# Prefix of counts formed in PSUM, the last tile stored in two halves, and a new static order of instructions

## The chip, the cores and the metric

The kernel runs on one core of a Trainium2 chip. A core has five engines with instruction queues of their own: PE (TensorE, matmuls, operands from SBUF, results into PSUM banks), DVE (VectorE), ACT (ScalarE), POOL (GpSimd) and SP, which here only issues DMAs. PEld in the profile is PE's weight load. The metric is the device time of one execution, in microseconds.

## The reference

Attention over 8 batches with 8 heads (sequence 256, head dimension 64), then a gated depthwise convolution with 15 taps and SiLU, added to the attention's output; the sum is the input of a mixture of experts with 2048 tokens, 4 groups of 4 experts, one expert per token:

```python
scores = (q @ k.T) / sqrt(D); attn = softmax(scores); x = (attn @ v)    # (8, 256, 512)
x_g = x * sigmoid(glu_gate)
conv = depthwise_conv15(x_g, conv_w)                                    # same padding
x = x + conv * sigmoid(conv)                                            # (2048, 512) tokens
g = argmax(x @ w_group); e = argmax(x @ w_expert[g])
out = g_w * e_w * (relu(x @ w1[g, e]) @ w2[g, e])                       # F = 1024
```

`g_w` and `e_w` are the softmax values of the two choices. All arrays are fp32.

## The kernel before

**Tiling.** The attention and convolution run as 16 units: 4 groups of 2 batches, by 4 blocks of 128 channels (2 heads). Per unit: `pair` forms the scores (L490) and the product with v (L510), `head` the maximum (DVE, L519), the exponential (ACT, L524) and the transposes (PE, L531), `tail` the division and the gate. Units 1 to 5 take their convolution on PE (`conv_pe`): SP fetches shifted copies of the gated input (DMAs at L616), and L626 multiplies them with diagonals; the others take 15 taps on DVE (L671).

**Routing.** When a group's four units are done, `route` forms the logits on PE (L763, copied to SBUF, then L771), DVE picks group and expert (L787 to L813, result `oh`), PE counts them over the batch (L819), and DVE finds the expert that most of the batch's tokens want (its number `ei` is read by SP at L860) and the tokens that want another one (`ohl_all`). For those a place in a list is needed: `cum` is the running sum of `ohl_all` over the group's four tiles of 128 tokens (L836, L838), and L840 and L841 turn it into ranks. Meanwhile `rows` transposes x and writes its token rows to DRAM.

**Experts.** `dense` runs each batch of 256 tokens through its majority expert: 8 pieces of weights of 512 KB (`loads`, L865, into `raw` buffers, 5 of them), each split into a high part (`wh`, L293 from `split`, on ACT or DVE) and a rest (`wl`, two halves at L888, on POOL or DVE), then 96 matmuls of 128x256 (L914) for the first layer, relu with the same split (`hidden`, L948 to L961: `hh`, and `hl` either on DVE or by `tm` on ACT and POOL), 48 matmuls of 128x512 in two token tiles (L935 to L937), and `store` (scale by the router's weight at L973 or L975, one DMA of 256 KB at L978). Tokens that want another expert go through `leftover`: gathered rows, weights in `gv` slots (L1249, 8 slots of 512 KB, shared with the attention's inputs), two layers (L1169, L1192), and an indirect DMA by POOL (L1201, `scatter`) that writes them over the rows in `out`. Since it must come last for its rows, a scatter and the stores of `out` are ordered by the program. What is left after that goes through a loop with a dynamic count at the end (L1294), which has no round in these runs.

**What sets the order.** The instructions are emitted by a planner (`Flow`) while the program is built. Every stage is a generator that asks for an engine with a booked length (`run`, `at`), for a buffer (`get`, `take`) or for a flag; `Flow` keeps a queue for each engine and emits the ready entry of lowest key, with a planned time of its own. `KEYS` shifts the keys of stages, `WAYS` says instance by instance which engine takes a step that several can do, `SW` is the price in the key for a change of the matmul's shape on PE, and the constants NSL to CMO are numbers of buffers and caps on banks. So the order on each engine is fixed at build time, and a booked length or a key can move anything. `UC` is the number of L914 matmuls that are booked at a time.

Of the kernel before, what the change touches and what calls it, by code (L numbers as in the profile page):

```python
# [17 lines left out]
P = 128  # L18
# [25 lines left out]
NU = NG * NC  # L44
NSL = 22
HB = 3
NQK = 2
NGV = 8
NRAW = 5
NW = 4  # L50
# [3 lines left out]
KP = -4  # L54
CD = 598.26, 74.86, 138.82, 696.08
UC = 6
DC = 0
NPRO = 5
SW = 0.51
CSC = 6  # L60
CS0 = 4
CAC = 5
CMO = 7
NAV = 1
NPT = 6
NPR = 6
EXIT = 0.095
# [4 lines left out]
PC = 1, 2, 3, 4, 5  # L72
WAYS = dict(kk='1012001112122021', pT='1001100110101001000011001000100100000000000010001000100001000111', rb='22020221102202', rc='111100111010101', x='01001111110011', xg='0000100000000011', t1='11000000111011', silu='2001002110111221', res='00001010111', xh='01011010100001', xl='00010011', xr='0000010000011111', xd='011100100011101', ls='1001', wh='11000101001010001', wl='01000010000000110011101001000111000000000000011000000000000000000000000000001', y='00000011000001', yd='000100011111111', tap='1222101010000111', sb='0100001110011011', ab='110010000111', hl='10111111111110110010100101000011')
KEYS = dict(kk=2.03, score=-8.59, av=26.22, max=-9.5, exp=0.07, pT=71.65, dn=0.56, rt=-0.29, rc=1.94, xg=-21.49, cp=-6.47, th=-1.41, sp=-0.92, apt=0.31, conv=-1.17, convb=2.57, res=-0.53, xh=57.76, xl=-0.81, rows=1.68, lt=0.52, ls=-1.05, wh=9.13, hh=-0.67, hr=3.64, hm=1.04, y=-1.31, yd=0.81)
BOTH = "convb kk rb xg res xh xl wh wl".split()
# [201 lines left out]
def flag(f):  # L277
    return "flag", f
# [7 lines left out]
def attn_conv_moe(ctx, tc, aQ, aG, cw, wr, wE, cst, out):  # L286
# [185 lines left out]
    def pair(u, i):  # L472
# [12 lines left out]
        nm = small.tile([P, 2, 2], F32, name="nm")  # L485
        yield at("score", 0, u.k + 0.1 * i, ("PE", 0.875))
        for qt in range(2):
# [17 lines left out]
        if fl.now[2] < u.tv:  # L505
            fl.now[2], fl.now[3] = u.tv, None
        yield at("av", 0, u.k + 0.1 * i, ("PE", 0.875))
        for kt in range(2):
# [36 lines left out]
    def tail(u):  # L545
# [9 lines left out]
        v_.reciprocal(dn, dn)  # L555
        e = yield at("rb", u.n, u.k, ("ACT", 0.1 + 0.21 * nb), ("DVE", 0.07 + 0.14 * nb), ("POOL", 0.5 * nb))
        copy(e, rb[:, 0:nb].rearrange("p u (m d) -> p (u m) d", m=4),
# [141 lines left out]
    def residual(u, acc, ia):  # L699
# [12 lines left out]
        u.xl = slot(u.nl, F32R, u)  # L712
        e = yield at("xl", u.n, -3, ("POOL", 0.1 + 0.53 * nb), ("DVE", 0.1 + 0.27 * nb))
        on[e].tensor_tensor(u.xl, x, u.xh.bitcast(F32), ALU.subtract)
# [36 lines left out]
    def route(G_):  # L751
# [16 lines left out]
        lp, cp, rp = rt[:, 0:TT * 20], rt[:, 80:80 + nb * NE], rt[:, 112:112 + (TT + 1) * NE]  # L768
        yield run("PE", 0.85)
        for t in range(TT):  # L770
# [68 lines left out]
        yield run("PE", 0.5)  # L839
        t_.matmul(rp[:, 0:TT * NE], lt_ex, ohl, start=True, stop=False, skip_group_check=True)  # L840
# [38 lines left out]
    def split(m, n, ir, raw):  # L879
# [5 lines left out]
        for h in range(2):  # L885
            sl = slice(h * DM, h * DM + DM)
            e = yield at("wl", 16 * m.b + 2 * n + h, -1, ("POOL", 1.24), ("DVE", 0.63))
            on[e].tensor_tensor(wl[:, sl], raw[:, sl], wh[:, sl].bitcast(F32), ALU.subtract)  # L888
# [4 lines left out]
    def dense():  # L893
        for m in ms:
# [4 lines left out]
            for n in range(4):  # L899
# [7 lines left out]
                for f in range(2):  # L907
                    k = 0
                    for ww, lo in ((w4h, 0), (w4h, 1), (w4l, 0)):
                        for c in range(NC):  # L910
                            if k % UC == 0:
                                yield run("PE", 0.12 * UC)
                            x = (xs[c].xl if lo else xs[c].xh)[:, m.i, :]
# [4 lines left out]
            if m.i == gr[m.g].nb - 1:  # L918
                for u in xs:
                    fl.back("sl", u.nh)  # L920
                    fl.back("sl", u.nl)
            iy = yield take("bk", 2, "mo", CMO + 2 * (att[0] == NU))
            ys = [flat(bank(j)) for j in iy]
            for j in range(4):
# [5 lines left out]
                for t in range(2):  # L930
                    sl = slice(t * P, (t + 1) * P)
                    for k in range(2):
                        if DC or k == 0:
                            yield run("PE", 0.71 if DC else 1.42)
                        t_.matmul(ys[t], hh[:, k, sl], w3h[:, k, :], start=j == 0 and k == 0, stop=False)  # L935
# [7 lines left out]
    def hidden(m, n, ib, hp):  # L943
# [20 lines left out]
        fl.set(m.h[n])  # L964

    def store(m, t, iy, yp):
        yield flag(gr[m.g].done)
        n = yield get("y")
        y = work.tile([P, DM], F32, name="y", bufs=2)
        tt = 2 * m.b + t  # L970
        w = yield at("y", tt, -5, ("ACT", 0.55), ("DVE", 0.62))
        if w == "ACT":
# [119 lines left out]
    def gather_all(os):  # L1092
# [4 lines left out]
        for t0 in range(0, TA, 4):  # L1097
# [7 lines left out]
            yield run("PE", 0.45)  # L1105
            for t in range(4):
# [101 lines left out]
    def first_tables():  # L1208
# [4 lines left out]
        n = yield take("bk", 1, "lo")  # L1213
        yield run("DVE", 5.1)
        tables_a(flat(bank(n)))
# [140 lines left out]
```

## Time and profile before

| | us |
|---|---|
| median of 3 runs (369.4 to 369.95) | 369.69 |
| profiled execution | 370.42 |
| its span | 368.6 |
| PE busy in it | 348.4 (95%) |
| POOL busy | 266.2 (72%) |
| DVE busy | 280.8 (76%) |
| ACT busy | 232.2 (63%) |

The mean granted clock of PE was 0.989 of full speed. Up to about 240 us the attention and convolution overlap with the first expert batches; from 240 to 306 the leftover tokens and expert batches share PE, and the DMA engines are at their fullest; from 306.6 on there are only expert batches, until the last matmul ends at about 362.15.

### The profile page before, as it was taken

The page shows a single profiled execution, that of the slowest core. Times are in us where ns is not written, and L with a number is a line of the kernel's source. Part 1 is how long each engine was busy: PE and PEld are TensorE (multiplying, and loading weights), DVE is VectorE, ACT ScalarE, POOL GpSimd, SP SyncE. Part 2 cuts the span into 40 slices and gives each one's busy share as a digit, 9 for nine tenths or more (in the row PEclk, how much of TensorE's full clock was granted, in tenths as well). Part 3 has the DMA queues.
Part 4 walks back from the last instruction along what each step waited for, and adds up shares of the span by engine and source line. Part 5 has one row for each costly group of instructions (what it writes and reads, how often), then busy time and mean ns, then how long its engine had stood idle before and what let it go on. Part 6 is the DMA issues. An engine that isn't in the chain of part 4 may idle for free.

```text
span 368.6 us, 7954 instructions
## 1 busy us (share of the span) xinstructions
PE 348.4 (95%) x2766; PEld 277.0 (75%) x2766; DVE 280.8 (76%) x557; ACT 232.2 (63%) x534; POOL 266.2 (72%) x264
## 2 busy tenths in 40 slices
PE   7999999989999996998999999799999999999993
PEld 6666357635798776977787788779988977998982
DVE  3899948895999999999999999999999647201100
ACT  3987678746998653557989887344556534555521
POOL 1664766355887773569995866798869996999891
PEclk9999999999999998999999999899999999999999
DMA  7737964899266452549534332548999965855401
GB/s 269 246 117 177 305 225 150 198 322 325 97 238 218 166 195 77 203 132 339 217 115 172 116 114 88 199 136 288 412 409 390 371 249 186 307 195 181 163 2 64
DMA packets 29084, 77.13 MB, mean 209 GB/s; under 512 B 2999, under 2 KB 3255, under 8 KB 29041
## 3 DMA queue, kind: packets, MB, share of 16 engines
q1 hardware_dynamic: 27008, 72.94, 57.6%
q10 hardware_dynamic: 1872, 3.41, 2.5%
q8 instruction: 24, 0.39, 0.4%
q0 software_dynamic: 160, 0.23, 0.2%
q14 instruction: 20, 0.16, 0.1%
HBM read 63.67 MB, written 7.54 MB: 193 GB/s over the span
## 4 chain that ended last, share of the span: by engine, by line
PE 53%; DVE 25%; ACT 8%; DMA 6%; issue 4%; SPq 1%; POOL 1%; DVEq 0%; ACTq 0%; POOLq 0%
PE bk L914 19%; DVE bk L671 7%; PE bk L935 5%; PE bk L937 5%; PE bk L936 5%; ACT pr L524 5%; DVE nm L519 3%; PE bk L490 3%; PE bk L531 3%; PE bk L510 3%; DVE wl L888 3%; DMA gv<-wE 3%; PE bk L626 2%; DMA gv<-aG 2%; DMA wl<-sl 2%
## 5 line engine op out<-in xcount | busy, mean ns | idle before, releaser
L888 POOL TENSOR_TENSOR wl<-raw,wh 128x512 fp32r<-128x512 f32 x113 | 145.3, 1311 | 12.4 <-ACT wh L293 11.6
L671 DVE SCALAR_TENSOR_TENSOR bk<-sl,cwq,bk 128x512 f32<-128x512 f32 x143 | 102.6, 747 | 1.3
L914 PE MATMUL bk<-sl,wh 128*128 128x256 f32 x512 | 79.2, 294 | 0.0
L293 ACT CAST wh<-raw 128x1024 fp32r<-128x1024 f32 x57 | 60.1, 1054 | 23.9 <-PE bk L937 11.7
L914 PEld LDWEIGHTS bk<-sl,wh 128*128 128x128 f32 x512 | 68.5, 195 | 5.3 <-issue 3.9
L524 ACT ACTIVATE pr<-bk,nm 128x256 f32<-128x256 f32 x128 | 59.4, 493 | 19.4 <-DVE nm L519 18.9
L935 PE MATMUL bk<-wh,hh 128*128 128x512 f32 x128 | 51.8, 405 | 0.0
L936 PE MATMUL bk<-wl,hh 128*128 128x512 f32 x128 | 50.6, 395 | 0.0
L937 PE MATMUL bk<-wh,hl 128*128 128x512 f32 x128 | 50.6, 395 | 0.0
L519 DVE TENSOR_REDUCE nm<-bk 128x2 f32<-128x512 f32 x64 | 40.1, 681 | 8.3 <-PE bk L490 8.2
L961 POOL TENSOR_TENSOR hl<-tm,hh 128x512 fp32r<-128x512 f32 x20 | 27.0, 1352 | 19.8 <-ACT tm L954 14.8
L914 PE MATMUL bk<-sl,wl 128*128 128x256 f32 x256 | 41.4, 285 | 0.0
L531 PE MATMUL bk<-c_id,pr 128*128 128x128 f32 x256 | 36.2, 278 | 4.1 <-ACT pr L524 4.0
L948 ACT ACTIVATE hh<-bk 128x512 fp32r<-128x512 f32 x32 | 19.3, 603 | 31.7 <-PE bk L914 21.8
L531 PEld LDWEIGHTS bk<-c_id,pr 128*128 128x128 f32 x256 | 28.2, 140 | 13.1 <-ACT pr L524 8.3
L914 PEld LDWEIGHTS bk<-sl,wl 128*128 128x128 f32 x256 | 35.6, 193 | 0.0
L490 PE MATMUL bk<-qk 64*128 64x256 f32 x256 | 32.9, 392 | 0.1
L510 PE MATMUL bk<-pT,gv 128*64 128x256 f32 x256 | 32.7, 388 | 0.0
L490 PEld LDWEIGHTS bk<-qk 64*128 64x128 f32 x256 | 23.4, 186 | 7.4 <-issue 4.4
L524 ACT ACTIVATION_READ_ACCUMULATOR pr<-bk,nm 128x1 f32 x128 | 28.8, 225 | 0.0
L935 PEld LDWEIGHTS bk<-wh,hh 128*128 128x128 f32 x128 | 24.1, 188 | 5.9 <-issue 0.8
L937 PEld LDWEIGHTS bk<-wh,hl 128*128 128x128 f32 x128 | 24.1, 188 | 5.8
(161 smaller groups left out, 550.5 us busy)
## 6 DMA issues: line engine op xcount, KB each, us to landing
raw<-wE SPq DMA_DIRECT2D x64, 512.0 KB, 4.5
gv<-wE SPq DMA_DIRECT2D x24, 512.0 KB, 10.0
gv<-aG SPq DMA_DIRECT2D x16, 512.0 KB, 5.7
qk<-aQ SPq DMA_DIRECT2D x15, 512.0 KB, 3.7
wh<-sl SPq DMA_DIRECT2D x10, 270.0 KB, 6.1
wl<-sl SPq DMA_DIRECT2D x10, 270.0 KB, 5.7
out_dram<-y SPq DMA_DIRECT2D x9, 256.0 KB, 4.4
out_dram<-y ACTq DMA_DIRECT2D x7, 256.0 KB, 3.0
```

The costliest lines, as they stand in the source:

```text
L293: (a_.copy if e == "ACT" else on[e].tensor_copy)(o, i)
L490: t_.matmul(scs[hh][:, qt, :], t[sl, i, qt * P:(qt + 1) * P], t[sl, i, 256:512], start=True, stop=True)
L510: t_.matmul(u.a[64 * hh:64 * hh + 64, i, :], u.vt[:, i, kt, hh, :], pTs[hh][1][:, kt, :], start=kt == 0, stop=kt == 1)
L519: v_.reduce_max(nm[:, hh, :], sc, axis=AX.X, negate=True)
L524: a_.activation(pr[:, qt, :], sc[:, qt, :], AF.Exp, bias=nm[:, hh, qt:qt + 1], scale=1.0, accum_out=u.sm[:, i, qt, hh, 0:1])
L531: t_.transpose(tp[:, kt, qt * P:(qt + 1) * P], pr[:, qt, kt * P:(kt + 1) * P], ident)
L671: v_.scalar_tensor_tensor(acc if k == KT - 1 else ac, x, w, acc if k == m and m > 1 else ac, ALU.mult, ALU.add)
L888: on[e].tensor_tensor(wl[:, sl], raw[:, sl], wh[:, sl].bitcast(F32), ALU.subtract)
L914: t_.matmul(hp[:, f, :], ww[:, f, c, :], x, start=k == 0, stop=k == 11)
L935: t_.matmul(ys[t], hh[:, k, sl], w3h[:, k, :], start=j == 0 and k == 0, stop=False)
L936: t_.matmul(ys[t], hh[:, k, sl], w3l[:, k, :], start=False, stop=False)
L937: t_.matmul(ys[t], hl[:, k, sl], w3h[:, k, :], start=False, stop=j == 3 and k == 1)
```

## The change

- `route`: the copy and the three adds of the running sum go into the routing's PSUM bank (`sums`), and one copy takes the result to SBUF as `cum`, which L841 (now L843) reads as before.
- `dense`: for the last 128 tokens (last batch, second tile) each 128x512 matmul becomes two of 128x256, one for each half of the columns, in banks of their own (three banks instead of two in the last batch). `half` scales the first half on DVE and stores it by SP, the second on ACT and by ACT's queue, 128 KB each.
- Buffers: `raw` 5 to 3, `gv` 8 to 10, slots for x (`NSL`) 22 to 23, exponentials (`NPR`) 6 to 4.
- The planner: `UC` 6 to 12, `SW` 0.51 to 75.59, the caps CSC and CAC, new `WAYS` and `KEYS`, and other booked lengths in some twenty places (the conv units' DMAs among them).

The units on PE are 1 to 5 in both. The core of the diff (lines of `KEYS` and `WAYS` cut):

```diff
-NSL = 22
+NSL = 23
...
-NGV = 8
-NRAW = 5
+NGV = 10
+NRAW = 3
...
-UC = 6
+UC = 12
...
-SW = 0.51
+SW = 75.59
-CSC = 6
+CSC = 5
...
-CAC = 5
+CAC = 2
...
-NPR = 6
+NPR = 4
...
-        yield run("SP", 2.4, -20)
+        yield run("SP", 4.3, -20)
...
-        fl.now[2] = max(fl.now[2] + 3.2, fl.land(1200))
+        fl.now[2] = max(fl.now[2] + 4.3, fl.land(1800))
...
-        yield run("DVE", 1.45)
+        yield run("DVE", 1.65)
...
         cum = small.tile([P, TT, NE], F32, name="cum")
-        v_.tensor_copy(cum[:, 0], ohl[:, 0])
+        sums = ps(0, TT, NE)
+        v_.tensor_copy(sums[:, 0], ohl[:, 0])
         for u in range(1, TT):
-            v_.tensor_tensor(cum[:, u], cum[:, u - 1], ohl[:, u], ALU.add)
-        yield run("PE", 0.5)
+            v_.tensor_tensor(sums[:, u], sums[:, u - 1], ohl[:, u], ALU.add)
+        v_.tensor_copy(cum, sums)
...
-            iy = yield take("bk", 2, "mo", CMO + 2 * (att[0] == NU))
+            iy = yield take("bk", 3 if m.b == B - 1 else 2, "mo", CMO + 2 * (att[0] == NU))
...
+                    if m.b == B - 1 and t == 1:
+                        if j == 3:
+                            yield get("y")
+                            y = work.tile([P, DM], F32, name="y", bufs=2)
+                        for h in range(2):
+                            yield run("PE", 0.71)
+                            c, yp = slice(h * S, h * S + S), ys[1 + h][:, 0:S]
+                            for k in range(2):
+                                t_.matmul(yp, hh[:, k, sl], w3h[:, k, c], start=j == 0 and k == 0, stop=False)
+                                t_.matmul(yp, hh[:, k, sl], w3l[:, k, c], start=False, stop=False)
+                                t_.matmul(yp, hl[:, k, sl], w3h[:, k, c], start=False, stop=j == 3 and k == 1)
+                            if j == 3:
+                                fl.go(half(m, h, c, y, yp), -5, fl.now[2], "PE")
+                        continue
...
+    def half(m, h, c, y, yp):
+        yield flag(gr[m.g].done)
+        tt = 2 * m.b + 1
+        yield run(("DVE", "ACT")[h], (0.35, 0.33)[h])
+        if h:
+            a_.activation(y[:, c], yp, AF.Copy, scale=rec[:, tt, 1:2])
+        else:
+            v_.tensor_scalar(y[:, c], yp, rec[:, tt, 1:2], None, ALU.mult)
+        w = ("SP", "ACT")[h]
+        yield run(w, 0.43)
+        on[w].dma_start(out=out[tt * P:(tt + 1) * P, c], in_=y[:, c])
```

How the order moves is shown at two places. The first is DVE's queue where the second group is routed; `L787` is its first step of the choice and `L671` are conv taps (numbers behind `bk` and `sl` name banks and slots). Before:

```order
L888 TENSOR_TENSOR wl<-raw,wh 128x512
L293 CAST wh<-raw 128x1024
L671 SCALAR_TENSOR_TENSOR bk_1631<-sl_995,cwq,bk_1631 128x512
L671 SCALAR_TENSOR_TENSOR bk_1765<-sl_1198,cwq,bk_1765 128x512
L671 SCALAR_TENSOR_TENSOR bk_1631<-sl_995,cwq,bk_1631 128x512
L787 TENSOR_REDUCE gmx<-bk_1767 128x4
```

and after, where `bk_1814` is the routing's bank and the copy is that of the logits:

```order
L671 SCALAR_TENSOR_TENSOR bk_1545<-sl_999,cwq,bk_1545 128x512
L293 COPY y<-bk_1814 128x512
L671 SCALAR_TENSOR_TENSOR acc<-sl_999,cwq,bk_1545 128x512
L671 SCALAR_TENSOR_TENSOR bk_1885<-sl_1205,cwq,bk_1885 128x512 x2
L787 TENSOR_REDUCE gmx<-bk_1814 128x4
```

A weight subtraction and a weight cast left this place on DVE, and the logits' copy came to it.

The second is the end of the program. On ACT, whose last work is the last y, before:

```order
L293 CAST wh<-raw 128x1024 x2
L948 ACTIVATE hh<-bk_4599 128x512
L954 ACTIVATE tm<-bk_4599 128x512
L973 ACTIVATE y<-bk_4632,rec 128x512
L973 ACTIVATE y<-bk_4633,rec 128x512
L978 DMA out_dram<-y 128x512
```

and after (`bk_4121` holds a leftover tile's second layer, `ys` its scaled rows):

```order
L964 ACTIVATE hh<-bk_4545 128x512
L293 CAST wh<-raw 128x1024
L1001 ACTIVATE y<-bk_4579,rec 128x512
L987 ACTIVATE y<-bk_4581,rec 128x256
L992 DMA out_dram<-y 128x256
L1225 ACTIVATE ys<-bk_4121,sws 128x128
```

On PE the same end, after (L942 to L944 are the half-width matmuls, L1220 is the leftover's second layer, L1192 before):

```order
L944 MATMUL bk_4581<-wh,hl 128x256
L942 MATMUL bk_4581<-wh,hh 128x256
L943 MATMUL bk_4581<-wl,hh 128x256
L944 MATMUL bk_4581<-wh,hl 128x256
L1220 MATMUL bk_4121<-gv,hT 32x128 x32
```

The last leftover product moved from ahead of the last group's routing to the end of PE's queue, behind the last tile's halves; its `ys` and the scatter are the last work of ACT and POOL, and the scatter waits there for the stores of the last tile.

## Rows read from the trace of the kernel before

**Rows 1.** The page's busy times: us, share of the span, instructions.

```profile
PE 348.4 (95%) x2766; PEld 277.0 (75%) x2766; DVE 280.8 (76%) x557; ACT 232.2 (63%) x534; POOL 266.2 (72%) x264
```

**Rows 2.** Windows: stretch, length, busy time of engines, clock, DMA share, GB/s.

```profile
240.00:306.60 66.60, 65.64 (x771) 57.35 (x770) 55.71 (x106) 33.28 (x50) 59.05 (x48) 1.00 0.82 312
306.60:362.20 55.60, 55.19 (x333) 48.46 (x332) 11.44 (x35) 26.00 (x34) 49.40 (x40) 1.00 0.51 172
```

**Rows 3.** Waits of PE: line, waited for, us in total, times, longest.

```profile
PE bk L531 <- ACT pr L524: 4.0, 8, 1.2
PE bk L819 <- DVE oh L813: 3.0, 2, 2.8
PE bk L841 <- DVE cum L838: 2.2, 2, 1.9
PE bk L626 <- DMA wh<-sl: 1.6, 2, 1.3
PE bk L378 <- POOL sm L432: 1.0, 1, 1.0
PE bk L1169 <- DMA gv<-wE: 1.0, 1, 1.0
```

**Rows 4.** Timeline: start, us, engine and line; in brackets idle time before, releaser.

```profile
137.59 1.76 DVE L293 CAST wh<-raw 128x1024 fp32r<-128x1024 f32 x1
139.28 2.06 DVE L671 SCALAR_TENSOR_TENSOR bk<-sl,cwq,bk 128x512 f32<-128x512 f32 x3
...
144.34 0.63 PE L819 MATMUL bk<-oh,c_sb 128*128 128x32 f32 x4 [2.79 <-DVE oh L813]
...
167.33 2.48 DVE L519 TENSOR_REDUCE nm<-bk 128x2 f32<-128x512 f32 x4
...
169.12 0.66 PE L531 MATMUL bk<-c_id,pr 128*128 128x128 f32 x4 [1.18 <-ACT pr L524]
...
230.02 2.63 DVE L838 TENSOR_TENSOR cum<-cum,ohl_all 128x16 f32<-128x16 f32 x3
```

**Rows 5.** Windows behind two of the waits; the third last number is the clock.

```profile
145.10:148.50 3.40, 3.40 (x17) 3.40 (x18) 3.19 (x10) 1.77 (x3) 2.83 (x3) 0.51 0.41 154
233.90:237.20 3.30, 3.30 (x18) 3.30 (x17) 2.88 (x15) 2.02 (x3) 2.09 (x2) 0.50 0.80 266
```

**Rows 6.** Groups by form: shapes and count, busy us, mean ns, idle before.

```profile
L838 DVE TENSOR_TENSOR cum<-cum,ohl_all 128x16 f32<-128x16 f32 x12 | 6.2, 517 | 0.4
L836 DVE COPY cum<-ohl_all 128x16 f32<-128x16 f32 x4 | 3.0, 754 | 0.1
L789 DVE TENSOR_TENSOR bk<-bk,c_sb 128x16 f32<-128x16 f32 x8 | 1.5, 182 | 0.3
```

**Rows 7.** DMA issues from 246 to 302, then from 306 to 350: median us to landing.

```profile
gv<-wE SPq DMA_DIRECT2D x24, 512.0 KB, 10.0
raw<-wE SPq DMA_DIRECT2D x11, 512.0 KB, 9.5
...
raw<-wE SPq DMA_DIRECT2D x16, 512.0 KB, 4.3
```

**Rows 8.** Groups by form, the cast and the subtraction of the weights.

```profile
L293 ACT CAST wh<-raw 128x1024 fp32r<-128x1024 f32 x57 | 60.1, 1054 | 23.9 <-PE bk L937 11.7 <-PE bk L914 3.5 <-POOL wl L888 3.4
L888 POOL TENSOR_TENSOR wl<-raw,wh 128x512 fp32r<-128x512 f32 x113 | 145.3, 1311 | 12.4 <-ACT wh L293 11.6 <-DVE wh L293 0.8
```

**Rows 9.** The chain that ended last: start, us, what.

```profile
301.01 1.89 PE bk L1192 x64
...
362.19 0.69 ACT y L973
```

**Rows 10.** DMA issues from 355 to 369: count, KB each, median us to landing.

```profile
out_dram<-y SPq DMA_DIRECT2D x1, 256.0 KB, 2.1
out_dram<-y ACTq DMA_DIRECT2D x1, 256.0 KB, 3.0
out_dram<-ys,ixs POOLq DMA_INDIRECT x1, 2.1
```

More of the change, by code (lines that the diff above doesn't have):

```diff
@@ L54 @@
 KP = -4
-CD = 598.26, 74.86, 138.82, 696.08
-UC = 6
+CD = 870.39, 381.01, 464.81, 600.18
+UC = 12
 DC = 0
 NPRO = 5
-SW = 0.51
-CSC = 6
+SW = 75.59
+CSC = 5
 CS0 = 4
-CAC = 5
+CAC = 2
 CMO = 7
@@ L72 @@
 PC = 1, 2, 3, 4, 5
[L73 to L74 removed]
+WAYS = dict(kk='1012020202222211', pT='110001011011000000100000011000000000010001000000000000000101', rb='1222022200022212', rc='10111001100001', x='001000000010001', xg='000111000100101', t1='0011000111111001', silu='0222211112120012', res='0011100000000001', xh='0110001000110001', xl='11010000111', xr='0101000100000011', xd='0111101011001111', ls='0101', wh='001000000000001', wl='11000000000100000000101000000000000010001010001001', y='01000000001', yd='1110100011111111', tap='21121401110041', sb='0000000001111111', ab='1000010001010111', hl='0101101100010110011001000000001')
+KEYS = dict(kk=-1.0, tg=-7.8, score=-78.01, max=-2.23, exp=1.28, tp=-4.53, pT=-0.08, rb=0.58, rt=-1.9, rc=0.58, x=-1.93, xg=0.96, cp=0.03, th=-5.5, sp=-1.16, apt=-2.18, conv=0.45, convb=-0.61, res=-15.34, xh=1.39, xl=-2.75, xr=-4.43, lt=0.67, wl=2.54, hh=2.67, hr=3.07, y=0.23, yd=0.26)
 BOTH = "convb kk rb xg res xh xl wh wl".split()
@@ L485, in pair @@
         nm = small.tile([P, 2, 2], F32, name="nm")
-        yield at("score", 0, u.k + 0.1 * i, ("PE", 0.875))
+        yield at("score", 0, u.k + 0.1 * i, ("PE", 0.87))
         for qt in range(2):
@@ L506, in pair @@
             fl.now[2], fl.now[3] = u.tv, None
-        yield at("av", 0, u.k + 0.1 * i, ("PE", 0.875))
+        yield at("av", 0, u.k + 0.1 * i, ("PE", 0.87))
         for kt in range(2):
@@ L555, in tail @@
         v_.reciprocal(dn, dn)
-        e = yield at("rb", u.n, u.k, ("ACT", 0.1 + 0.21 * nb), ("DVE", 0.07 + 0.14 * nb), ("POOL", 0.5 * nb))
+        e = yield at("rb", u.n, u.k, ("ACT", 0.1 + 0.21 * nb), ("DVE", 0.07 + 0.14 * nb), ("POOL", 0.28 * nb))
         copy(e, rb[:, 0:nb].rearrange("p u (m d) -> p (u m) d", m=4),
@@ L712, in residual @@
         u.xl = slot(u.nl, F32R, u)
-        e = yield at("xl", u.n, -3, ("POOL", 0.1 + 0.53 * nb), ("DVE", 0.1 + 0.27 * nb))
+        e = yield at("xl", u.n, -3, ("POOL", 0.1 + 0.57 * nb), ("DVE", 0.1 + 0.27 * nb))
         on[e].tensor_tensor(u.xl, x, u.xh.bitcast(F32), ALU.subtract)
@@ L768, in route @@
         lp, cp, rp = rt[:, 0:TT * 20], rt[:, 80:80 + nb * NE], rt[:, 112:112 + (TT + 1) * NE]
-        yield run("PE", 0.85)
+        yield run("PE", 0.82)
         for t in range(TT):
@@ L816, in route @@
         o4 = oh.rearrange("p (i t) e -> p t i e", i=nb)
-        yield run("PE", 0.5)
+        yield run("PE", 0.4)
         for t in range(2):
@@ L835, in route @@
         cum = small.tile([P, TT, NE], F32, name="cum")
-        v_.tensor_copy(cum[:, 0], ohl[:, 0])
+        sums = ps(0, TT, NE)
+        v_.tensor_copy(sums[:, 0], ohl[:, 0])
         for u in range(1, TT):
-            v_.tensor_tensor(cum[:, u], cum[:, u - 1], ohl[:, u], ALU.add)
-        yield run("PE", 0.5)
+            v_.tensor_tensor(sums[:, u], sums[:, u - 1], ohl[:, u], ALU.add)
+        v_.tensor_copy(cum, sums)
+        yield run("PE", 0.42)
         t_.matmul(rp[:, 0:TT * NE], lt_ex, ohl, start=True, stop=False, skip_group_check=True)
@@ L886, in split @@
             sl = slice(h * DM, h * DM + DM)
-            e = yield at("wl", 16 * m.b + 2 * n + h, -1, ("POOL", 1.24), ("DVE", 0.63))
+            e = yield at("wl", 16 * m.b + 2 * n + h, -1, ("POOL", 1.25), ("DVE", 0.63))
             on[e].tensor_tensor(wl[:, sl], raw[:, sl], wh[:, sl].bitcast(F32), ALU.subtract)
@@ L911, in dense @@
                             if k % UC == 0:
-                                yield run("PE", 0.12 * UC)
+                                yield run("PE", 0.1185 * UC)
                             x = (xs[c].xl if lo else xs[c].xh)[:, m.i, :]
@@ L931, in dense @@
                     sl = slice(t * P, (t + 1) * P)
+                    if m.b == B - 1 and t == 1:
[12 more added lines that the diff above has]
+                        continue
                     for k in range(2):
                         if DC or k == 0:
-                            yield run("PE", 0.71 if DC else 1.42)
+                            yield run("PE", 0.705 if DC else 1.41)
                         t_.matmul(ys[t], hh[:, k, sl], w3h[:, k, :], start=j == 0 and k == 0, stop=False)
@@ L970, in store @@
         tt = 2 * m.b + t
-        w = yield at("y", tt, -5, ("ACT", 0.55), ("DVE", 0.62))
+        w = yield at("y", tt, -5, ("ACT", 0.58), ("DVE", 0.65))
         if w == "ACT":
@@ L1104, in gather_all @@
                              io32.unsqueeze(1).broadcast_to([P, 4, m]), ALU.is_equal)
-            yield run("PE", 0.45)
+            yield run("PE", 0.62)
             for t in range(4):
@@ L1213, in first_tables @@
         n = yield take("bk", 1, "lo")
-        yield run("DVE", 5.1)
+        yield run("DVE", 5.5)
         tables_a(flat(bank(n)))
```

## Prediction

> **What bounds the kernel now.** I read the busy times first: TensorE (PE) is busy 95% of the span, VectorE (DVE) 76%, ScalarE (ACT) 63% [rows 1]. By stretches, PE has 65.64 us of work in the 66.6 us from 240 to 306.6 and 55.19 in the 55.6 after that [rows 2]. PE's instructions are the same before and after but for 24 matmuls that become 48 of half the width, so time can only come from PE's waits, from stretches at the lower clock, and from the tail behind the last matmul. The waits of PE are the second view: eight groups, 13.4 us in all, the six of a microsecond or more in [rows 3]. The third view is the granted clock: behind the wait of 2.79 us at 144.34 [rows 4] and behind the longest wait for `cum`, 1.9 us [rows 3], the clock reads 0.51 and 0.50 for 3.40 and 3.30 us, with PE busy throughout [rows 5]. That is the 1.2 GHz level, and half of each stretch is lost: 3.4 us. Behind the waits of 1.0 to 1.3 us no such stretch follows. So 13.4 + 3.4 = 16.8 us is the most that a better order could give back ahead of the tail.
>
> **The change part by part.**
>
> *Routing, the choice of the expert.* In the second group's routing PE waits 2.79 us for `oh`. The timeline shows why [rows 4]: the logits are there at about 137.8, and DVE then has the cast of 1.76 us (from 137.59) and three conv taps (2.06 us) to end before it can start on the choice at 141.3, some 3.4 us late. In the new order the cast is gone from that place; behind the copy of the logits stand three taps alone, and they run while PE still folds the logits (L771). 1.76 us of cast go, and some 0.6 of the taps come under L771: 2.4 of the 2.79. The other `oh` wait (3.0 - 2.79 = 0.2) goes with it. Term: **-2.6**. The cast isn't lost: ACT takes five more of 1.05 us each [rows 8], spread over the run, and it is idle 37% of it.
>
> *Prefix of counts.* Before, `cum` is a copy of 754 ns and three adds of 517 ns, by the means, in SBUF [rows 6]; the three took 2.63 us in the third group's routing [rows 4], where L841 waits 1.9. After, copy and adds write PSUM. The nearest row is L789, the same shape, with one operand and the result in a bank: 182 ns [rows 6]. With 0.2 for each of the two copies it is 0.2 + 3 x 0.18 + 0.2 = 0.9 us against 2.3 by the means and about 3.4 in the third group: 1.4 to 2.5 us less. From the other side: adds of 517 ns kept and a copy put on top, +0.2. I take L789's value, since engine, shape and places are the same. L841 waits 2.2 us in two routings; PE also has somewhat more rows between L819 and this matmul than before in every routing. Term: **-2.2**.
>
> *The clock.* Both half-clock stretches come behind these two waits, so they go with them: **-3.4**; nothing, if new waits of that length appear elsewhere.
>
> *Conv units on PE.* Their matmuls wait 1.6 us in two places for the shifted copies that SP fetches [rows 3]. The planner now books 4.3 us of SP for them and a landing at least 4.3 us off, instead of 2.4 and 3.2, and in the new order each unit's first L626 stands behind 1 to 6 us more PE work than before. Term: **-1.4**, 0.2 kept.
>
> *Leftover weights.* Ten `gv` slots for eight, and the leftover matmuls stand 5 to 10 us of PE work later. The one wait for them is 1.0 us [rows 3]. Term: **-1.0**. The two slots more let 512 KB loads start earlier in a stretch where a load takes 10.0 us to land already [rows 7]; that is weighed with the raw buffers.
>
> *Softmax.* L531 waits 4.0 us in eight places [rows 3], the longest, at 169.12, for an exponential that stood behind 2.48 us of maxima on DVE [rows 4]. DVE has fewer weight casts (7 to 2), fewer weight subtractions (15 to 10), a shorter prefix, and more of `hl` (12 to 20). I take a quarter: **-1.0**, bounds 0 and -2.
>
> *Three raw buffers for five.* A piece of weights goes load, cast on ACT (1.05), two subtractions on POOL (2 x 1.31) [rows 8], then its buffer is free. With 9.5 to 10 us of landing between 246 and 302 [rows 7] a round trip is 10 + 1.05 + 2.6 + 0.5 = 14.2 us, or 4.7 a piece with three buffers; the eight pieces of that stretch have 5.1 us of PE work each to hide under by the new order. So it costs nothing while the round trip is under 15.4 us, and then about 8 / 3 = 2.7 us for each microsecond. After 306 a load lands in 4.3 [rows 7]: 8.5 / 3 = 2.8 us a piece, about what POOL needs anyway. Term: 0; it is the main rival.
>
> *The last tile.* Before, the last matmul ends at about 362.15, and 6.4 us follow: ACT's y (0.69 us from 362.19) [rows 9], the store (3.0 us from issue to landing) [rows 10], 2.7 to the program's end. After, its columns come as two halves of 128 KB, scaled by DVE and ACT, stored by SP and ACT. PE's work for it stays (as many columns), and the third bank that it takes is free, attention being over; were it not, PE would wait for one y, 0.69. And the last leftover product, 1.89 us of PE that stood at 301.01 [rows 9], now stands behind all dense matmuls, its `ys` and its scatter last of all. The scatter waits on POOL, with no work queued behind it, for the landing of the last y stores. So the dense part ends 1.9 us sooner, and behind it come 0.1, half a y (between half of 0.69 and all of it: 0.5), a store, the scatter (2.1) [rows 10] and the 2.7. The store of a half lies between 1.5 (half of 3.0) and 3.0; I take 2.7, near the rows of whole tiles, since none shows time falling with size. 0.1 + 0.5 + 2.7 + 2.1 + 2.7 = 8.1, less 1.9 is 6.2, against 6.4. Term: **-0.2**, bounds -1.4 and +0.1.
>
> Here rows and a rule part. The two 256 KB stores at the end land 2.1 and 3.0 us after their issue [rows 10], so the rows leave open what a half costs. The Trainium skill (DMA: Bandwidth & Descriptors, section "Anatomy of one DMA — SWDGE (gpsimd) path") fits a transfer as about 2.0 us fixed plus bytes at 436 GB/s, which makes a half 2.3 us by estimate, so that splitting brings next to nothing. By that fit the tail's term is -0.6 instead of -0.2, and the forecast 0.4 lower. It is fitted on a software queue, and these stores go by hardware queues, so the rows stand.
>
> *New waits.* Choices and keys change for every stage, so the whole order is new. Bounds: no wait, and as much as the old order had, 16.8. Where they will lie the trace of before can't show; the measure I take is what the old order had apart from routing, conv and leftover loads (L531 4.0, L378 1.0): **+5**.
>
> **Sum.** -2.6 - 2.2 - 3.4 - 1.4 - 1.0 - 1.0 - 0.2 + 5 = -6.8. The profiled execution took 370.42 us, so 363.6; it lay 0.73 above the median of the runs, 369.69, so **362.9**.
>
> **The rivals.**
>
> *The waits come back elsewhere.* For it: DVE is the busiest engine behind PE, and its queue decides most of the waits. Against it: the largest have causes that the new order removes. With 12 for 5 the sum is +0.2: 369.9, no change.
>
> *Slower: three raw buffers starve PE in the stretch full of loads.* Place: 246 to 302, where `gv` and `raw` loads share the DMA engines, 82% busy over the wider window [rows 2, 7]; ten `gv` slots put more of them ahead of each raw load. It decides from a round trip of 15.4 us; at 18.5 it costs 3.1 x 2.7 = 8.4 us, and a half-clock stretch that such waits bring 1.7: 362.9 + 8.4 + 1.7 = 373.0. Against it: fewer loads in flight land sooner.
>
> *A new long wait, and the clock behind it.* The first dense chunk of the first group now stands behind 10 us of PE work from L819, where it had 18. The expert's number must be formed and read by SP, then the load takes 4.3 or more, the cast 1.05, a subtraction 1.31 [rows 7, 8]: 6.7 and what the number takes. A wait of 2 us and a half-clock stretch are 3.7: 366.6.
>
> *The prefix in PSUM is no faster.* Then L841's 2.2 and one half-clock stretch stay: +3.9, 366.8.
>
> **How the numbers follow.** The forecast, 355.7 to 367.5: 0.60. Waits come back, around 369.9: 0.13 (0.04 faster, 0.05 the same, 0.04 slower). Raw buffers, 371 to 377: 0.14. Long wait: 0.09, prefix: 0.04, both faster. The low end is the sum with no new waits, 357.9, and the lower bounds of the softmax and tail terms, 2.2 less. The high end, 371, takes in the first rival and the mildest of the second. Faster 0.60 + 0.04 + 0.09 + 0.04 = 0.77; same 0.05; slower 0.18. Within 0.2% (0.74 us) a measurement can't tell this kernel from no change.
>
> **What would show it.** PE's wait at the second group's L819 under 0.6 us, and for `cum` under 0.4 in every routing; copies and adds of `cum` under 0.25 us each; no window at half clock after 100; no wait of L626 over 0.5; the last y store landing 2.1 to 3.0 us after its issue, and the scatter right behind it. I am wrong if landing, cast and subtractions of a raw piece exceed 15.4 us between 240 and 300 and PE waits for `wh` or `wl` there, or if PE's waits come to more than 10 us again.

## The result, and the profile after

The changed kernel takes 358.04 us (median of 4 runs, 357.0 to 360.25) against 369.57 for the kernel before: a ratio of 0.9695, 95% interval 0.9648 to 0.9741. The forecast was 362.9 with a range of 355.7 to 371.0; the sign and the range held, and the gain was 11.5 us where 6.8 were forecast.

The busy times of the profiled execution (358.33 us, span 356.6), to be held against [rows 1]:

```profile
PE 342.7 (96%) x2790; PEld 272.1 (76%) x2790; DVE 268.9 (75%) x554; ACT 236.7 (66%) x537; POOL 257.6 (72%) x257
```

PE's busy time itself fell by 5.7 us, though it has the same work but for the last tile's halves. The waits of PE in the changed kernel, against [rows 3] (line, waited for, total, times, longest):

```profile
PE bk L531 <- ACT pr L524: 2.7, 8, 1.0
PE bk L1135 <- DVE y L1131: 1.1, 1, 1.1
PE bk L378 <- POOL sm L432: 1.0, 1, 1.0
PE bk L1153 <- DMA xs<-x_rows,ix: 0.9, 1, 0.9
PE bk L490 <- POOL qk L442: 0.8, 1, 0.8
PE bk L916 <- ACT pT L293: 0.3, 1, 0.3
```

The waits for `oh`, for `cum`, for the conv copies and for `gv` are gone; four new ones came, 3.1 us in all. No stretch at half clock lies ahead of the last matmul. That isn't these two executions alone: the granted clock averages 0.989 over 19 runs of the kernel before, 0.997 and 0.996 over four and five of the changed one, and 0.008 of the span is 3 us. The books of PE, from the two traces ("idle" is time with neither matmul nor weight load; L626 is the conv on PE, from each matmul's start to the next one's, idle taken out):

| us | before | after | difference |
|---|---|---|---|
| idle | 12.7 | 6.2 | -6.4 |
| lost to the half clock | 3.4 | 0 | -3.4 |
| L626 | 21.9 | 17.9 | -4.0 |
| all other work of PE | | | +1.7 |
| last matmul to the end of the span | 6.4 | 6.6 | +0.2 |
| span | 368.6 | 356.6 | -12.0 |

(The rows are rounded one by one.)

The 4 us at L626 are the part that the forecast had not seen. The five units have 160 of these matmuls, each with a quarter of the array's columns, so that four can run at a time (the timeline below has four that start within 0.2 us). One unit of 32 matmuls in the kernel before, in a window with L626's instructions alone (start and end, length, PE busy, PEld busy, clock, DMA share, GB/s):

```profile
80.60:87.10 6.50, 6.09 (x32) 1.83 (x32) 1.00 1.02 358
```

and one unit in the changed kernel:

```profile
75.50:79.40 3.90, 3.64 (x32) 0.94 (x32) 1.00 1.01 305
```

The same 32 matmuls keep PE busy for 6.09 us or for 3.64. Before, the timeline shows why (start, us, instruction, idle before):

```profile
80.65 1.04 PE L626 MATMUL bk<-wh,wd 128*32 128x512 f32 x2 [1.26 <-DMA wh<-sl]
81.37 1.05 PE L626 MATMUL bk<-wl,wd 128*32 128x512 f32 x2
82.72 1.05 PE L626 MATMUL bk<-wh,wd 128*32 128x512 f32 x2 [0.30 <-DMA wh<-sl]
83.43 0.62 PE L626 MATMUL bk<-wl,wd 128*32 128x512 f32 x1
83.43 0.62 PE L626 MATMUL bk<-wh,wd 128*32 128x512 f32 x1
83.44 0.62 PE L626 MATMUL bk<-wl,wd 128*32 128x512 f32 x1
83.60 0.59 PE L626 MATMUL bk<-wh,wd 128*32 128x512 f32 x1
```

Each of the four shifted copies feeds one column group. The first two groups start when their copies have landed, one after the other, and from then on the fours stay out of step. PE counts as busy meanwhile, so the list of waits shows 2.0 us and hides the rest.

### The profile page after: what moved, and what is told of

It reads as the page before. It is cut to its first block, busy times and chain, and to the rows that moved or that the text cites. A ratio compares the mean times of both kernels' runs of the same rounds, so it can differ in the third digit from the quotient of the medians.

```text
span 356.6 us, 7988 instructions
## 1 busy us (share of the span) xinstructions
PE 342.7 (96%) x2790; PEld 272.1 (76%) x2790; DVE 268.9 (75%) x554; ACT 236.7 (66%) x537; POOL 257.6 (72%) x257
## 5 line engine op out<-in xcount | busy, mean ns | idle before, releaser
L890 POOL TENSOR_TENSOR wl<-raw,wh 128x512 fp32r<-128x512 f32 x118 | 153.7, 1328 | 26.2 <-ACT wh L293 24.2
L671 DVE SCALAR_TENSOR_TENSOR bk<-sl,cwq,bk 128x512 f32<-128x512 f32 x137 | 99.8, 747 | 2.0
L293 ACT CAST wh<-raw 128x1024 fp32r<-128x1024 f32 x62 | 65.4, 1055 | 41.9 <-DMA raw<-wE 34.4
L916 PE MATMUL bk<-sl,wh 128*128 128x256 f32 x512 | 73.3, 286 | 0.4 <-ACT pT L293 0.3
L524 ACT ACTIVATE pr<-bk,nm 128x256 f32<-128x256 f32 x128 | 60.2, 488 | 15.6 <-DVE nm L519 15.4
L916 PEld LDWEIGHTS bk<-sl,wh 128*128 128x128 f32 x512 | 65.1, 189 | 4.1 <-issue 2.3
L952 PE MATMUL bk<-wl,hh 128*128 128x512 f32 x120 | 47.8, 398 | 0.1
L953 PE MATMUL bk<-wh,hl 128*128 128x512 f32 x120 | 47.4, 395 | 0.0
L973 DVE SCALAR_TENSOR_TENSOR hl<-bk,hh 128x512 fp32r<-128x512 f32 x20 | 13.7, 687 | 36.6 <-ACT hh L964 36.6
L531 PE MATMUL bk<-c_id,pr 128*128 128x128 f32 x256 | 38.5, 280 | 2.8 <-ACT pr L524 2.7
L916 PE MATMUL bk<-sl,wl 128*128 128x256 f32 x256 | 40.6, 281 | 0.0
L531 PEld LDWEIGHTS bk<-c_id,pr 128*128 128x128 f32 x256 | 28.1, 141 | 15.0 <-ACT pr L524 8.2
L916 PEld LDWEIGHTS bk<-sl,wl 128*128 128x128 f32 x256 | 34.6, 189 | 0.0
L293 ACT COPY pT<-bk 128x512 f32<-128x512 f32 x50 | 29.7, 604 | 2.0 <-PE bk L531 1.6
L703 POOL TENSOR_TENSOR sl<-sl,acc 128x512 f32<-128x512 f32 x12 | 15.8, 1317 | 15.7 <-DVE acc L636 7.7
```

The costliest lines, as they stand in the source:

```text
L293: (a_.copy if e == "ACT" else on[e].tensor_copy)(o, i)
L524: a_.activation(pr[:, qt, :], sc[:, qt, :], AF.Exp, bias=nm[:, hh, qt:qt + 1], scale=1.0, accum_out=u.sm[:, i, qt, hh, 0:1])
L531: t_.transpose(tp[:, kt, qt * P:(qt + 1) * P], pr[:, qt, kt * P:(kt + 1) * P], ident)
L671: v_.scalar_tensor_tensor(acc if k == KT - 1 else ac, x, w, acc if k == m and m > 1 else ac, ALU.mult, ALU.add)
L916: t_.matmul(hp[:, f, :], ww[:, f, c, :], x, start=k == 0, stop=k == 11)
L952: t_.matmul(ys[t], hh[:, k, sl], w3l[:, k, :], start=False, stop=False)
```

## The experiments

The first five kernels are the kernel before with edits that leave the order of the work as it was (the one cast apart). The kernel before took 368.92 us (median of 19 runs) beside the first four of them, 368.68 (7 runs) beside the fifth.

**The running sum in PSUM, alone.**

```diff
-        v_.tensor_copy(cum[:, 0], ohl[:, 0])
+        sums = ps(0, TT, NE)
+        v_.tensor_copy(sums[:, 0], ohl[:, 0])
         for u in range(1, TT):
-            v_.tensor_tensor(cum[:, u], cum[:, u - 1], ohl[:, u], ALU.add)
+            v_.tensor_tensor(sums[:, u], sums[:, u - 1], ohl[:, u], ALU.add)
+        v_.tensor_copy(cum, sums)
```

> The kernel before with only the running sum formed in PSUM (copy and three adds there, one copy to SBUF); the order on every engine stays as before. Theory A (the wait for cum and the half-clock stretch behind it are one thing, and both go): the adds take about 0.18 us each instead of 0.52, PE's wait for cum falls from 2.2 us in all to under 0.3, no half-clock stretch at 234: 2.0 + 1.7 less, about 366. Theory B (the wait goes but the clock falls there anyway): 2 less, about 367.6. Theory C (what is saved there is lost at the next wait): within 1 us of before.

364.69 us (ratio 0.9883, 0.9826 to 0.994): 4.2 less, theory A. The wait for `cum` is gone from the list, and so is the half-clock stretch at 234; the one at 145 stays. The list is also shorter by 1.1 us at L531 and 1.0 at the leftover's weights, so the 4.2 isn't those two terms alone. The groups by form of this kernel, against [rows 6] (busy us, mean ns, idle before):

```profile
L839 DVE TENSOR_TENSOR bk<-bk,ohl_all 128x16 f32<-128x16 f32 x12 | 2.2, 182 | 0.4
L840 DVE COPY cum<-bk 128x64 f32<-128x64 f32 x4 | 0.9, 224 | 0.1
L837 DVE COPY bk<-ohl_all 128x16 f32<-128x16 f32 x4 | 0.7, 178 | 0.1
```

An add takes the 182 ns of L789, and the chain about 1 us. The changed kernel has the same durations.

**One cast from DVE to POOL, alone.**

```diff
-        copy(e, wh, raw)
+        copy("POOL" if 8 * m.b + n == 12 else e, wh, raw)
```

> The kernel before with one weight cast, the one that DVE does ahead of the second group's choice of expert, done by POOL instead, which is idle 4.6 us there; the rest of the order stays. Theory A (the cast makes PE's wait for oh, and a wait of 1 us doesn't bring the half clock): the wait of 2.79 us falls to about 1.0, no half-clock stretch at 145: 1.8 + 1.7 less, about 366. Theory B (the clock falls there anyway): 367.8. Theory C (lost again later): within 1 us of before.

366.72 us (0.996, 0.9926 to 0.9993): 2.2 less by the medians, 1.5 by the ratio, between the theories. PE's wait for `oh` fell from 2.79 to 0.87, as expected, but the waits of this kernel show where it went:

```profile
PE bk L841 <- DVE cum L838: 4.3, 3, 2.1
PE bk L531 <- ACT pr L524: 4.3, 8, 1.4
PE bk L626 <- DMA wh<-sl: 1.5, 1, 1.5
PE bk L819 <- DVE oh L813: 1.1, 2, 0.9
```

The wait for `cum` comes up 2.1 us long in the same routing, where it had been covered by the longer wait ahead, so PE's idle time falls by 0.6 us only, from 12.7 to 12.1. And in this execution both half-clock stretches are gone, though PE still waits 2.08 us (up to 148.66) and 1.89 us (up to 231.4) for `cum`: the tie between a wait of about 2 us and the half clock, on which the forecast put 3.4 us, isn't a rule. Nor is their absence the kernel's own: its ten runs have mean clocks from 0.984 to 0.998, and the profiled one has the 0.998; the 19 runs of the kernel before have 0.983 to 0.996.

**Both.**

> The kernel before with both the running sum in PSUM and the one cast moved to POOL. Theory A (two separate causes, each with its half-clock stretch): the sum of the two runs, about 7 less, 362.5. Theory B (the two hide each other): no more than the larger of the two, about 366.

362.56 us (0.9818, 0.977 to 0.9867): 6.4 less, the sum of the two by the medians. The 95% interval reaches from 4.9 to 8.5, which is too wide to show that the two simply add up. But neither hides the other, as theory B had it: the wait for `cum` is gone from this kernel's list, and that for `oh` is 0.9 at most. Two small edits in the old order give more than half of the change's gain.

**The conv matmuls without their copies, alone, and with both edits.**

```diff
-        iv = [i.rearrange("p (b f) -> p b f", f=XW) for i in (t[:, 0:XW * nb] for t in im)]
+        iv = [xg[:, 0:nb, :] for t in im]
```

> The kernel before, but the conv matmuls of the five units on PE (L626) read the gated input in SBUF instead of the shifted copies, whose DMAs are still issued: no wait for them can arise. The convolution of these units, and what follows from it, isn't the reference's. The order on every engine stays. Theory A (the late copies cost more than PE's idle time, since L626's matmuls on four column groups of the array then run one after another instead of together): the matmuls at L626 take 17.9 us in all instead of 21.9, and PE's waits for wh and wl there (2.0) go: 6 less, about 363.6. Theory B (only the idle time counts, as the prediction had it): 2 less, about 367.6. Theory C (absorbed by later waits for weights): within 1 us of before.

The edit leaves out the shifts of the convolution and keeps the number and shape of its matmuls.

367.77 us (0.9967, 0.994 to 0.9994): 1.2 less, nearest to theory C. L626 fell to 17.9 us and its waits went, as theory A has it, so the lost overlap is real; but PE then waits 2.5 us at L568, and two stretches at half clock (88.6 to 92 and 143.2 to 150) cost 5.1 us where one of 1.7 had been.

> The kernel before with the running sum in PSUM, the one cast on POOL, and the conv matmuls reading SBUF instead of the shifted copies (the convolution of the five units on PE isn't the reference's). Theory A (with the routing waits out of the way, the lost overlap of the conv matmuls comes out as time): L626 takes 17.9 instead of 22.5 us, its wait of 0.6 goes: 5 less than the kernel with the first two edits (362.6), so 357.6, the time of the changed kernel. Theory B (as with the conv edit alone, DVE's residual step and the clock take it back): 361 to 362.5.

362.31 us (0.9833, 0.9774 to 0.9892): no different from the kernel with the two edits, theory B. Its timeline shows what takes the gain back:

```profile
84.12 0.63 ACT L440 ACTIVATE qk<-qk 128x512 f32<-128x512 f32 x1 [5.36 <-DMA qk<-aQ]
86.07 0.63 ACT L455 ACTIVATE gv<-gv 128x512 f32<-128x512 f32 x1 [1.32 <-DMA gv<-aG]
...
87.27 0.58 ACT L634 ACTIVATE sl<-bk 128x512 f32<-128x512 f32 x1
...
87.88 0.69 DVE L636 SCALAR_TENSOR_TENSOR acc<-sl,bk 128x512 f32<-128x512 f32 x1 [4.05 <-ACT sl L634]
...
88.71 1.09 PE L568 MATMUL bk<-c_id,rb 128*128 128x128 f32 x4 [4.08 <-DVE acc L636]
```

ACT stands before two loads of the next unit's inputs, in a stretch where the DMA engines are full; behind them in its queue is the step of the conv unit (L634), behind that DVE's, and PE's next matmul in the old order waits for it. By these traces the late conv copies had merely covered this. In the changed kernel PE has the first group's experts to do there:

```profile
82.39 0.66 PE L531 MATMUL bk<-c_id,pr 128*128 128x128 f32 x4
82.87 1.21 PE L916 MATMUL bk<-sl,wh 128*128 128x256 f32 x8
83.92 0.63 PE L916 MATMUL bk<-sl,wl 128*128 128x256 f32 x4
```

The first L916 runs at 82.87, the first L914 of the kernel before at 92.4. So the 4 us at L626 paid little in the old order, 1.2 alone and 0.3 behind the two edits; that they pay in the new one because PE has other work at that place is read from the traces, and no run takes that work away.

The next four start from the changed kernel. It took 358.77 us (5 runs, 0.9735, 0.9715 to 0.9756) beside three of them.

> The changed kernel itself, unaltered, as the measure for the other three of this set: about 358.0, PE's waits about 6.8 us, no half-clock stretch before the last matmul.

**The running sum back in SBUF.** The diff is that of the first experiment, reversed; the booking stays.

> The changed kernel with the running sum formed in SBUF again, in its booked place; all else stays. In the new order PE comes to the matmul on cum 0.7 to 1.8 us after cum is there. Theory A (the new order has covered most of the chain, so that the PSUM prefix and the order are two ways to the same gain): 1.3 to 2.3 us more on each chain leave waits of 0.3 to 1.0 us in each of the four routings, 2 us in all, 360. Theory B (the prefix is worth here what it is worth in the order before): 4 us more, 362. Theory C (fully covered): no change.

365.1 us (0.9888, 0.9862 to 0.9914): 6.3 more, beyond theory B. The waits:

```profile
PE bk L531 <- ACT pr L524: 3.0, 9, 1.0
PE bk L1133 <- DVE y L1129: 2.6, 1, 2.6
PE bk L841 <- DVE cum L838: 2.6, 2, 1.6
PE bk L568 <- DVE sg L853: 1.1, 1, 1.1
```

2.6 us at `cum` are near theory A's 2. The rest is what follows: DVE is late behind the routing, at L853 (1.1) and at the leftover's tables (2.6 instead of 1.2), and a half-clock stretch of 3.4 us comes at 251. By the groups of instructions, the copies and adds of `cum` take 10.0 us of DVE in the four routings instead of 3.8, and the new order has so little slack for DVE that these 6.2 us cost about as much. In the old order the same exchange was worth 4.2 us; the two intervals overlap, so a difference between the orders isn't shown.

This run also shows what made the adds slow. One chain of it, DVE and POOL:

```profile
145.35 1.30 POOL L714 TENSOR_TENSOR sl<-sl,sl 128x512 fp32r<-128x512 f32 x1
145.46 3.69 DVE L838 TENSOR_TENSOR cum<-cum,ohl_all 128x16 f32<-128x16 f32 x3
146.60 1.29 POOL L580 TENSOR_TENSOR sl<-sl,rb 128x512 f32<-128x512 f32 x1
147.84 1.27 POOL L975 TENSOR_TENSOR hl<-tm,hh 128x512 fp32r<-128x512 f32 x1
```

Each of the three adds takes as long as POOL's instruction beside it, about 1.2 us. All twelve of this kernel, by its source view (ns: shortest, median, longest), then the twelve of the changed kernel:

```profile
L838 DVE TENSOR_TENSOR cum<-cum,ohl_all x12: 174/1163/1223, 73.8 to 301.9; 128x16 f32<-128x16 f32 x12
```

```profile
L839 DVE TENSOR_TENSOR bk<-bk,ohl_all x12: 182/182/183, 73.2 to 294.1; 128x16 f32<-128x16 f32 x12
```

In the kernel before, four adds took 1.19 to 1.21 us, each beside a POOL instruction, and eight took 0.17 to 0.18 with POOL idle: the mean of 517 ns in [rows 6] is a mixture. Undisturbed, the add in SBUF is no slower than in PSUM; the change takes it out of POOL's way. The Trainium skill (SBUF — State Buffer, section "Who interferes with whom") has VectorE and GpSimd share one pair of SBUF ports as an exclusive lock, for which a VectorE instruction with two SBUF inputs contends and one with at most one SBUF input doesn't; that agrees with 1.2 us beside POOL, and with 182 ns where one operand lies in PSUM.

**The last leftover product back ahead of the experts.**

```diff
-            yield run("PE", 1.75, shape="c")
+            yield run("PE", 1.75, shape="n" if self is ls_[-1] else "c")
```

> The changed kernel with the last leftover product booked without the price for a change of shape, so that the planner puts it back behind the last group's routing; its scatter then runs among the last weight subtractions. Theory A (the end of the program hangs on store, then scatter): the dense part ends 1.9 us later, but behind it come only half a y, a store of 1.9 and 2.7: about 1.3 less, 356.7. Theory B (POOL, which subtracts weights there, is held up by the scatter, and PE waits for wl): no gain, 358 to 359.

360.35 us (0.979, 0.9759 to 0.9821): not faster; theory A falls. Its profiled execution has a half-clock stretch at 11 us, ahead of anything that the edit moves, and its six runs average a clock of 0.992 where the five of the unaltered kernel have 0.996, which is about 1.7 us, as much as it is slower. So I compare from the last routing's matmul on `cum` on: 61.3 us to the end of the span, against 60.8 and 61.3 in the two profiled executions of the unaltered kernel. From that matmul the dense part ends 2.0 to 2.5 later (1.9 of it the product), and 1.9 to 2.0 come back behind it. The reason is PE's own queue. Its instructions at the loop's line, in this kernel (durations in ns: shortest, median, longest):

```profile
L1322 PEldq COMPARE_BRANCH  x3: 101/193/3868, 350.4 to 357.6; - x3
L1322 ACTq COMPARE_BRANCH  x3: 37/38/54, 353.8 to 356.3; - x3
```

and in the kernel before:

```profile
L1294 PEldq COMPARE_BRANCH  x3: 101/193/3488, 360.1 to 367.1; - x3
L1294 ACTq COMPARE_BRANCH  x3: 38/38/54, 363.9 to 366.6; - x3
```

The branch over the loop takes PE 3.5 to 3.9 us, from just behind its last matmul, and the others 0.04 to 0.06. From PE's last matmul to the end it is 6.4 us in the kernel before and in this one, 6.6 in the changed kernel: what is stored before that branch ends costs nothing that these traces show, and moving work from ahead of PE's end to PE's end gains nothing. What PE waits for there the list doesn't say, but the DMA packets do: in each of the 14 traces a 16 KB transfer of the kind "instruction" starts 0.9 to 1.6 us after this branch, and the branch ends 1.4 to 1.6 us after that transfer. So it looks like PE fetching the code behind the loop; no run here tests it.

**The last tile whole.** The half-width matmuls are whole again, in the same place, with one y on ACT and one store by ACT's queue.

```diff
-                            c, yp = slice(h * S, h * S + S), ys[1 + h][:, 0:S]
-                            for k in range(2):
-                                t_.matmul(yp, hh[:, k, sl], w3h[:, k, c], start=j == 0 and k == 0, stop=False)
...
+                            k, yp = h, ys[1]
+                            t_.matmul(yp, hh[:, k, sl], w3h[:, k, :], start=j == 0 and k == 0, stop=False)
...
+                            if j == 3 and h:
+                                fl.go(half(m, 1, slice(0, DM), y, yp), -5, fl.now[2], "PE")
```

> The changed kernel with the last tile whole again: 24 matmuls of 128x512, one y on ACT, one store of 256 KB by ACT's queue. Theory A (a half lands sooner because it is smaller, and the scatter behind it too): the y takes 0.2 more and the store 0.4 to 1.2 more, of which 0.1 is covered by the leftover product: 0.5 to 1.3 more, about 359. Theory B (a store's time is nearly all fixed): 0.2 more at most, 358.2.

360.08 us (0.9784, 0.9753 to 0.9815), 1.3 above the unaltered one, though its runs spread from 358.3 to 362.46 and average a clock of 0.992 against 0.996, about 1.6 us. Its profiled execution, at 0.995, took 358.3, no more than the unaltered kernel's. The stores at the end of its trace:

```profile
out_dram<-y SPq DMA_DIRECT2D x1, 256.0 KB, 2.1
out_dram<-y ACTq DMA_DIRECT2D x1, 256.0 KB, 3.0
out_dram<-ys,ixs POOLq DMA_INDIRECT x1, 2.1
```

and of the changed kernel's:

```profile
out_dram<-y SPq DMA_DIRECT2D x1, 256.0 KB, 2.1
out_dram<-y SPq DMA_DIRECT2D x1, 128.0 KB, 1.9
out_dram<-y ACTq DMA_DIRECT2D x1, 128.0 KB, 1.7
out_dram<-ys,ixs POOLq DMA_INDIRECT x1, 2.5
```

The last store takes 3.0 us whole and 1.7 in half, and the scatter waits for it: it starts 2.8 us behind PE's last matmul instead of 1.3, and the span ends 7.3 us behind it instead of 6.4 and 6.6. So the halves are worth 0.7 to 0.8 us at the end of the trace, as theory A has it, because the scatter hangs on them. That they land sooner because they are smaller isn't shown. On SP's queue 256 KB took 2.1 us and 128 KB 1.9, and in the kernel with the product moved a half on ACT's queue took more than a whole tile here:

```profile
out_dram<-y ACTq DMA_DIRECT2D x1, 128.0 KB, 3.2
```

In that kernel 135 of its 144 packets were over by 354.17, and the last nine ran from 354.75 on, when a 16 KB transfer of instructions (353.83 to 354.76) had ended. The slow store of the whole tile overlaps such a transfer, too, and the half in 1.7 us doesn't: part of the 1.3 us is where the store falls. The Trainium skill (DMA: Bandwidth & Descriptors, section "Anatomy of one DMA — SWDGE (gpsimd) path") has about 2.0 us as the fixed part of a DMA on the software path; the halves, on hardware queues, landed in 1.7 and 1.9 altogether, so for these stores the measurement decides against it.

The last three kernels ran beside the kernel before at 368.68 us, like the fifth.

**The old booking of the conv copies, and one other entry of the tables.**

```diff
-        yield run("SP", 4.3, -20)
+        yield run("SP", 2.4, -20)
...
-        fl.now[2] = max(fl.now[2] + 4.3, fl.land(1800))
+        fl.now[2] = max(fl.now[2] + 3.2, fl.land(1200))
```

> The changed kernel with the old booking of the conv units' copies (2.4 us of SP, landing at 3.2 and 1200 KB); the planner lays out the order anew. Theory A (the booking is what keeps the conv matmuls from starting on half the copies): L626 takes 19.5 us or more, PE waits 0.5 us or more for wh and wl, the total is 2 to 5 more, 361 to 363. Theory B (other entries of the new tables place them): L626 stays at 17.9 to 18.3, and the total is what a new order happens to give.

395.62 us (1.0734, 1.0695 to 1.0773). L626 takes 19.0 us, and PE waits 1.0 for its copies, somewhat as theory A has it, but that is 2 of 37 us. Some 17 us of PE's work run at half clock. The waits of its trace, the four largest groups of 30 us idle in all:

```profile
PE bk L531 <- ACT pr L524: 11.4, 16, 3.5
PE bk L763 <- DVE sl L703: 4.2, 1, 4.2
PE bk L490 <- DVE pos L1039: 2.7, 1, 2.7
PE bk L952 <- POOL wl L890: 2.2, 1, 2.2
```

```diff
-WAYS = dict(kk='1012020202222211', ...)
+WAYS = dict(kk='1112020202222211', ...)
```

> The changed kernel with one entry of the tables altered: the scaling of the second unit's k goes from POOL to DVE, and the planner lays out all that follows anew. Theory A (prefix, buffers and bookings carry the gain, and any order planned with them keeps it): 357 to 360, the first wait for qk shorter by 0.8. Theory B (the gain hangs on this one order): 361 to 366, with waits of PE of 9 us or more.

383.92 us (1.0412, 1.0384 to 1.044), theory B and far beyond it: PE is idle for 20.6 us, and 15 us of its work run at half clock. One step of the second unit on another engine shifts everything that is planned after it. The tables and the bookings fit one order: with one booking or one entry undone and the rest kept, the whole gain is lost and more. What undoing one of them costs in the same order can't be told from these two runs.

**Four raw buffers under the same order.**

```diff
-    wraw = ctx.enter_context(tc.tile_pool(name="wraw", bufs=NRAW))
+    wraw = ctx.enter_context(tc.tile_pool(name="wraw", bufs=4))
```

> The changed kernel with four raw buffers allocated while the planner still counts three, so that the order stays and only the waits of loads for a free buffer relax. Theory A (three buffers cost PE nothing, as no wait for wh or wl shows): 358 to 359. Theory B (they hold the casts up and, through them, PE): 1 us or more less, 357 or under.

357.47 us (0.9698, 0.9665 to 0.973), the lowest of all, but its interval overlaps those of the changed kernel (0.9648 to 0.9741 and 0.9715 to 0.9756): no difference shown, so the three buffers cost nothing that these runs can tell. That fits the changed kernel's loads between 240 and 300, against [rows 7]:

```profile
gv<-wE SPq DMA_DIRECT2D x24, 512.0 KB, 9.1
raw<-wE SPq DMA_DIRECT2D x12, 512.0 KB, 6.5
```

A raw load lands in 6.5 us where it took 9.5, and a round trip is some 11 us, well under the 15.4 from which three buffers would stall PE.

## Why the forecast held, and where it missed

- **Choice of the expert, -2.6.** Right, 3.0 by the list. The cast was the main cause: the run that moves it alone takes 1.9 off this wait. What I hadn't seen is that it covered another one, for `cum`, of 2.1 us, so that alone it gives PE little.
- **Prefix, -2.2.** Right, to the tenth by the list; an add takes 182 ns. The reason is another than that "engine, shape and places are the same": SBUF isn't slower by itself, POOL's work beside it made it so. In the changed kernel the prefix is worth 6.3 us, with what follows on DVE, against 4.2 in the old order.
- **Half clock, -3.4.** The size is right. The reason given, that the stretches follow those two waits, is only half shown: with the sum in PSUM alone one stretch went with its wait, but with the cast moved both were missing in the profiled execution while two waits of 1.9 and 2.1 us stayed.
- **Conv units, -1.4.** The step that failed. I took the price from the list of waits, 1.6 us, where the cost was 2.0 idle plus 4.0 of L626 out of step inside PE's busy time: 6.0. That time "can only come" from waits, the clock and the tail was wrong, too, for that reason.
- **Leftover weights, -1.0.** Right; the two new waits in the leftover's tables and gather, 2.0, belong to the new ones.
- **Softmax, -1.0.** 1.3 by the list.
- **Three raw buffers, 0,** and the rival that rested on them: no wait for `wh` or `wl` in the list, and the round trip fell instead of rising.
- **Last tile, -0.2.** +0.2 measured, and by another mechanism: the end hangs on PE's last instruction and its slow branch, within which store and scatter just fit. The halves landed in 1.7 and 1.9 us, below the 2.7 in the sum and outside the 2.1 to 3.0 that the forecast named as its sign. They matter by 0.7 to 0.8 because the scatter was put behind them; the leftover's move gains nothing, and the run that undoes it doesn't either.
- **New waits, +5.** 3.1, and 1.7 more for work of PE that takes slightly longer in the new order (scores and logits by about 1 us each), which I hadn't counted. That the two come to nearly 5 is luck: the 5 was read off the old order's waits.
- **The rival of a long wait at the first expert chunk.** The chunk stands at 82.87 without a wait; its early place is, by the traces, what lets the conv gain through.

By the terms, the forecast was short by 4.6 at the conv and 1.9 at the new waits, and over by 1.7 at PE's other work.

## What to carry to other kernels

A mean over one form can mix two cases: look at the shortest and the longest of the group before taking it as a price. A list of waits undercounts a late operand where small matmuls share the array: compare the busy time of the same matmuls between two places, and look for fours that run as twos. Before pricing a removed wait, look one step on along the same queues: here one wait covered another of its own size, and the conv copies covered a load of inputs, so in the old order their gain didn't come out as time. One profiled execution can have a clock that the next run of the same kernel doesn't have: compare the granted clocks of all runs before giving a stretch at half clock to an edit. With a planner, an edit that leaves the order alone tells what one cause is worth; one that replans tells how far the order is from another one, here 25 to 37 us.

## What the hardware showed beyond that

- PE's branch over the dynamic loop took 3.4 to 4.2 us in the 14 traces where the other engines' takes 0.05, and ended 1.4 to 1.6 us behind a 16 KB transfer of instructions. The span ended 6.4 to 6.9 us after the last matmul in 13 of them, and 7.3 in the one whose scatter landed after the branch.
- A wait's length doesn't tell whether the half clock follows: 3.5 us at 94 in the kernel with the old booking brought none, waits of 1.9 and 2.1 in the profiled execution of the kernel with the cast moved neither, while 2.0 in the kernel with four raw buffers (at 242) was followed by 3.4 us of it, and so were 1.5 us at 9.3, just behind waits of 1.0 and 0.3, in the kernel with the product moved. What decides stays open here.
- A 128x16 add between two SBUF operands took 0.17 us with POOL idle and 1.2 beside POOL's 128x512 operations on two SBUF operands, seven times as much; with one operand in PSUM it took 0.18 in all twelve cases.
